# Feed-forward layers of a fused attention kernel: five nearly equal token blocks, and second products begun two tiles into the next block

## The chip, the cores and the metric

The kernel runs on one core of a Trainium2 chip. The metric is the time of one execution in device microseconds (us); the kernel before takes 1122.49 us, the median of 3 runs (1120.99 to 1125.56).

## The reference

Causal attention with per-position decay (4 batches, 8 heads, 576 positions, 64 wide) gives x, 2304 tokens by 512. Two feed-forward layers follow, all in float32:

```
def _moe_ref(x, w_in, w_out):            # w_in 512 x 2048, w_out 2048 x 512
    h = x @ w_in
    g = h * (1.0 / (1.0 + np.exp(-1.702 * h)))
    return g @ w_out

def _moe2_ref(x, w_gate, w_val, w_out):  # 512 x 1536, 512 x 1536, 1536 x 512
    g = x @ w_gate
    silu = g * (1.0 / (1.0 + np.exp(-g)))
    return silu * (x @ w_val) @ w_out
```

## The kernel before, in words

Attention comes first and is ordered by a planner of its own (class `Program`); the change does not touch it. The feed-forward layers are the function `moe`. There the tokens are the moving columns of each matmul, cut into five blocks, and the 128 x 128 weight pieces are stationary. A float32 operand is split into a high and a low part, so each product is three matmuls (lines 512 to 514: high x high, high weight x low, low weight x high).

The hidden features are cut into tiles of 128 and the tiles into chunks: four chunks of four tiles in layer 1, four of three in layer 2. For each chunk and each block the loop at line 579 runs over the chunk's tiles. A tile is a `first` product (line 516: 12 matmuls in layer 1; in layer 2 two of them, 24 matmuls), then the gate (line 529: ACT's tanh into `t`, DVE's multiplication into `s`), in layer 2 one more multiplication (line 546), and `split_g` (line 522: ACT's cast gives the high part of `g`, DVE's subtraction the low part). When all tiles of a block are made, the block is kept in `pend`. Its second products, `flush` (line 568), run inside the next block: 48 matmuls in layer 1, 36 in layer 2, in four groups by output tile `d`, each group followed on DVE by an addition to `acc` (lines 557 and 559). PE's order inside a flush may mix the four groups.

Weights arrive as float64 or float32 bit patterns and are converted on the way (`load_w`, line 449): ACT line 461, four DVE steps (lines 463 to 468), ACT's cast (line 481) and POOL's subtraction (line 482) give a `w` tile of a high and a low part. There are 13 such tiles; `pump` moves the conversions forward between tiles and flush groups, and a weight's place comes free when its last reader is done. A last block's flush frees the second weights of its chunk.

The lines that set when a flush runs are these:

```
for i in range(c, e):
    gs.append(layer1(i, t0, n) if lay == 1 else layer2(i, t0, n))
    ...
    if pend is not None:
        flush(pend)
        pend = None
    pump()
```

So PE has one tile of the next block as cover between the end of a block's last tile and the first use of its `g`.

Of the kernel before, what the change touches and what calls it, by code (L numbers as in the profile page):

```python
# [7 lines left out]
F32 = mybir.dt.float32  # L8
F32R = mybir.dt.float32r
# [99 lines left out]
def kernel(  # L109
# [13 lines left out]
    NW = 13  # L123
    NWA = 5
    NSTG = 3
    blocks = [(0, 512), (512, 512), (1024, 256), (1280, 512), (1792, 512)]

    def f32(ap):
        return ap.bitcast(F32)

    def pool(stack, name, bufs, **kw):
        return stack.enter_context(tc.tile_pool(name=name, bufs=bufs, **kw))
# [290 lines left out]
    def chunks(sizes):  # L423
        c = 0
        for n in sizes:
            yield c, c + n
            c += n
# [56 lines left out]
    def pump(force=False):  # L484
        for g in list(pipe):
            if next(g, "end") == "end":
                pipe.remove(g)
        if plan and len(pipe) < NSTG and (force or work[0] >= due[plan[0]]):
            pipe.append(load_w(plan.pop(0)))
            next(pipe[-1])  # L490

    def need(*keys):
        while not all(k in wt for k in keys):
            pump(True)

    def drop(*keys):
        for k in keys:
            del wt[k]
            live[0] -= 1

    def moe():
        gp = pool(ctx, "gp", 5, reuse_waits="tile")
        tp = pool(ctx, "tp", 2, reuse_waits="tile")
        ps = pool(ctx, "ps", 8, reuse_waits="tile", **psum)
        mp = pool(ctx, "mp", 1, reuse_waits="tile")
        acc = [mp.tile([128, KD, n], F32, name=f"acc{i}") for i, (_, n) in enumerate(blocks)]

        def mm3(o, pairs):
            n = len(pairs)
            work[0] += 3 * n * o.shape[1]  # L510
            for i, (wh, wl, rh, rl) in enumerate(pairs):
                nc.tensor.matmul(o, wh, rh, start=i == 0, stop=False)  # L512
                nc.tensor.matmul(o, wh, rl, start=False, stop=False)  # L513
                nc.tensor.matmul(o, wl, rh, start=False, stop=i == n - 1)  # L514

        def first(w, t0, n):
            o = ps.tile([128, 512], F32, tag="ps", name="ps")
            mm3(o[:, 0:n], [(w[:, 0, k * 128:(k + 1) * 128], w[:, 1, k * 128:(k + 1) * 128],
                             xhi[:, k, t0:t0 + n], xlo[:, k, t0:t0 + n]) for k in range(KD)])
            return o[:, 0:n]  # L520

        def split_g(s):
            n = s.shape[1]
            g = gp.tile([128, 2, 512], F32R, tag="g", name="g")
            nc.scalar.copy(out=g[:, 0, 0:n], in_=s)  # L525
            nc.vector.tensor_tensor(out=g[:, 1, 0:n], in0=s, in1=f32(g[:, 0, 0:n]), op=ALU.subtract)  # L526
            return g

        def gated(o, scale):
            n = o.shape[1]  # L530
            t = tp.tile([128, 512], F32, tag="t", name="t")[:, 0:n]
            nc.scalar.activation(out=t, in_=o, func=AF.Tanh, scale=scale)  # L532
            s = tp.tile([128, 512], F32, tag="s", name="s")[:, 0:n]
            nc.vector.scalar_tensor_tensor(out=s, in0=t, scalar=1.0, in1=o, op0=ALU.add, op1=ALU.mult)  # L534
            return s

        def layer1(i, t0, n):
            need(("w1", i))
            return split_g(gated(first(wt["w1", i], t0, n), 0.851))

        def layer2(i, t0, n):
            need(("wg", i), ("wv", i))
            g_ = first(wt["wg", i], t0, n)
            v_ = first(wt["wv", i], t0, n)
            s = gated(g_, 0.5)
            nc.vector.tensor_tensor(out=s, in0=s, in1=v_, op=ALU.mult)  # L546
            return split_g(s)

        def second(name, c0, gs, bi, d, mode):
            t0, n = blocks[bi]  # L550
            o = ps.tile([128, 512], F32, tag="ps", name="ps")[:, 0:n]
            ds = slice(d * 128, (d + 1) * 128)
            mm3(o, [(wt[name, c0 + i][:, 0, ds], wt[name, c0 + i][:, 1, ds], g[:, 0, 0:n], g[:, 1, 0:n])
                    for i, g in enumerate(gs)])
            a = acc[bi][:, d, :]
            if mode == "first":
                nc.vector.tensor_scalar(out=a, in0=o, scalar1=0.5, scalar2=None, op0=ALU.mult)
                return
            nc.vector.scalar_tensor_tensor(out=a, in0=o, scalar=0.5, in1=a, op0=ALU.mult, op1=ALU.add)  # L559
            if mode == "x":  # L560
                nc.scalar.copy(out=xhi[:, d, t0:t0 + n], in_=a)
                nc.vector.tensor_tensor(out=xlo[:, d, t0:t0 + n], in0=a, in1=f32(xhi[:, d, t0:t0 + n]), op=ALU.subtract)
            elif mode == "out":
                nc.sync.dma_start(out=out[ds, t0:t0 + n], in_=a)

        pend = None

        def flush(p):
            name, c0, gs, bi, mode, keys = p
            need(*[(name, c0 + i) for i in range(len(gs))])  # L570
            for d in range(KD):
                second(name, c0, gs, bi, d, mode)
                pump()
            if keys:
                drop(*keys)

        for lay, ff, sizes, name2 in ((1, FF1, CH1, "w1o"), (2, FF2, CH2, "w2o")):
            for c, e in chunks(sizes):
                for bi, (t0, n) in enumerate(blocks):
                    lastb = bi == len(blocks) - 1  # L580
                    gs = []
                    for i in range(c, e):
                        gs.append(layer1(i, t0, n) if lay == 1 else layer2(i, t0, n))
                        if lastb:
                            if lay == 1:
                                drop(("w1", i))
                            else:
                                drop(("wg", i), ("wv", i))
                        if pend is not None:
                            flush(pend)  # L590
                            pend = None
                        pump()
                    mode = "first" if c == 0 else "mid" if e < ff else "x" if lay == 1 else "out"
                    pend = (name2, c, gs, bi, mode, [(name2, i) for i in range(c, e)] if lastb else None)
        flush(pend)
# [18 lines left out]
    for _ in range(3):  # L614
        pump()
    moe()


# [48 lines left out]
```

## Time and profile before

| | before |
|---|---|
| median of 3 runs | 1122.49 us |
| the profiled execution, device time | 1123.12 us |
| its span in the trace | 1121.1 us |
| first and last matmul of the feed-forward layers start at | 265.77 and 1116.96 us |
| busy: PE, DVE, ACT, POOL | 94%, 56%, 32%, 16% of the span |

The span is the time from the first to the last instruction; the device time holds some 2 us around it. Matmuls are pipelined: one that lasts 0.39 us in a row is followed by the next after 0.23 us. So a loss on PE is read from the starts of two matmuls and the number of matmuls between them, not from busy time. A bracket at a row's end gives the time for which the engine sat idle before the row and what ended it.

### The profile page before, as it was taken

The numbers are of one execution on the slowest core, as the hardware profiler recorded it, in microseconds if no ns is written. First come the engines' busy times: TensorE is split into PE (matmuls) and PEld (weight loads), VectorE is DVE, ScalarE is ACT, GpSimd is POOL, SyncE is SP. The second block draws the span as 40 slices with busy tenths as digits, with TensorE's granted clock in tenths as the row PEclk, the third lists the DMA queues.
The fourth block names the chain that finished last, engine by engine and source line by source line (L and its number), as shares of the span: only waits on it lengthen the run. The fifth ranks groups of instructions, "written<-read, shape, count | busy, mean of one in ns | idle before, by whom it ended". The sixth has DMA issues, their size and how long they took to land.

```text
span 1121.1 us, 15630 instructions
## 1 busy us (share of the span) xinstructions
PE 1048.3 (94%) x6212; PEld 860.2 (77%) x6212; DVE 623.2 (56%) x1227; ACT 360.8 (32%) x648; POOL 182.4 (16%) x262
## 2 busy tenths in 40 slices
PE   2888777889999999999999999999999999999998
PEld 1666656667688788878877888888888888888886
DVE  5456756552966835664485578337733863363333
ACT  1455444443524313332343343123212321221110
POOL 4333343331201100200020011002100210010000
PEclk9999888999999999999999999999999999999999
DMA  3133353210221300220021012002200220000101
GB/s 121 45 103 114 97 165 105 96 47 23 79 72 38 113 1 1 75 75 1 19 95 37 1 57 95 1 1 77 93 1 1 88 82 1 1 0 29 48 19 75
DMA packets 25464, 61.43 MB, mean 55 GB/s; under 512 B 7760, under 2 KB 8272, under 8 KB 25392
## 3 DMA queue, kind: packets, MB, share of 16 engines
q1 hardware_dynamic: 25392, 60.45, 17.0%
q8 instruction: 48, 0.79, 0.3%
q14 instruction: 24, 0.20, 0.1%
HBM read 55.35 MB, written 4.94 MB: 54 GB/s over the span
## 4 chain that ended last, share of the span: by engine, by line
PE 80%; DVE 12%; ACT 2%; issue 2%; DMA 2%; POOL 1%; SPq 1%; ACTq 0%; DVEq 0%; POOLq 0%
PE ps L513 22%; PE ps L514 22%; PE ps L512 22%; PE sc L326 5%; PE xx L356 4%; PE mx L272 2%; DVE cvt L466 2%; DVE junk L279 2%; PE xx L385 2%; DVE cvt L468 2%; PE mx L275 1%; DVE cvt L464 1%; DVE cvt L463 1%; DVE g L526 1%; DVE s L534 1%
## 5 line engine op out<-in xcount | busy, mean ns | idle before, releaser
L512 PE MATMUL ps<-xhi,w 128*128 128x512 f32 (+1 forms) x800 | 294.5, 368 | 0.0
L513 PE MATMUL ps<-xlo,w 128*128 128x512 f32 (+1 forms) x800 | 294.4, 368 | 0.0
L514 PE MATMUL ps<-xhi,w 128*128 128x512 f32 (+1 forms) x800 | 294.2, 368 | 0.0
L513 PE MATMUL ps<-g,w 128*128 128x512 f32 (+1 forms) x560 | 207.5, 371 | 3.1 <-DVE g L526 3.1
L512 PE MATMUL ps<-g,w 128*128 128x512 f32 (+1 forms) x560 | 206.1, 370 | 3.7 <-ACT g L525 3.6
L514 PE MATMUL ps<-g,w 128*128 128x512 f32 (+1 forms) x560 | 206.1, 368 | 0.5 <-POOL w L482 0.5
L482 POOL TENSOR_TENSOR w<-cvt,w 128x512 fp32r<-128x512 f32 x68 | 89.4, 1319 | 664.8 <-ACT w L481 648.4
L532 ACT ACTIVATE t<-ps 128x512 f32<-128x512 f32 (+1 forms) x140 | 77.5, 554 | 298.4 <-PE ps L514 297.5
L512 PEld LDWEIGHTS ps<-xhi,w 128*128 128x128 f32 x800 | 150.8, 189 | 25.2
L514 PEld LDWEIGHTS ps<-xhi,w 128*128 128x128 f32 x800 | 150.8, 188 | 25.1
L513 PEld LDWEIGHTS ps<-xlo,w 128*128 128x128 f32 x800 | 150.8, 189 | 24.9
L534 DVE SCALAR_TENSOR_TENSOR s<-t,ps 128x512 f32<-128x512 f32 (+1 forms) x140 | 88.4, 631 | 123.9 <-ACT t L532 123.0
L525 ACT CAST g<-s 128x512 fp32r<-128x512 f32 (+1 forms) x140 | 81.0, 578 | 182.9 <-DVE s L546 129.4
L513 PEld LDWEIGHTS ps<-g,w 128*128 128x128 f32 x560 | 105.6, 189 | 24.5 <-DVE g L526 7.4
L512 PEld LDWEIGHTS ps<-g,w 128*128 128x128 f32 x560 | 105.4, 189 | 24.6 <-ACT g L525 7.3
L559 DVE SCALAR_TENSOR_TENSOR acc<-ps,acc 128x512 f32<-128x512 f32 (+1 forms) x120 | 76.0, 636 | 84.9 <-PE ps L514 84.2
L526 DVE TENSOR_TENSOR g<-s,g 128x512 fp32r<-128x512 f32 (+1 forms) x140 | 92.0, 658 | 54.1 <-ACT g L525 53.4
L514 PEld LDWEIGHTS ps<-g,w 128*128 128x128 f32 x560 | 105.6, 189 | 17.9 <-POOL w L482 0.9
L279 DVE CUSTOM_DVE_ANT_0 junk<-mx,maskw 128x512 bf16<-128x512 f32 (+3 forms) x128 | 61.8, 483 | 38.2 <-PE mx L275 36.2
L331 ACT ACTIVATE p<-sc 128x512 f32<-128x512 f32 (+2 forms) x128 | 56.4, 504 | 34.9 <-PE sc L326 34.6
L335 POOL TENSOR_SCALAR_AFFINE_SELECT p<-p 128x128 f32<-128x128 f32 (+1 forms) x160 | 43.9, 290 | 144.7 <-ACT p L331 143.6
L546 DVE TENSOR_TENSOR s<-s,ps 128x512 f32<-128x512 f32 (+1 forms) x60 | 38.0, 633 | 46.0 <-PE ps L514 45.7
(70 smaller groups left out, 1029.5 us busy)
## 6 DMA issues: line engine op xcount, KB each, us to landing
raw<-in_kq_dram SPq DMA_DIRECT2D x16, 576.0 KB
stg<-in_w_dram SPq DMA_DIRECT2D x16, 512.0 KB
stg<-in_w1o_dram SPq DMA_DIRECT2D x16, 512.0 KB
stg<-in_wg_dram SPq DMA_DIRECT2D x12, 512.0 KB
stg<-in_wv_dram SPq DMA_DIRECT2D x12, 512.0 KB
stg<-in_w2o_dram SPq DMA_DIRECT2D x12, 512.0 KB
vr<-in_v_dram SPq DMA_DIRECT2D x16, 320.0 KB
rb<-rw SPq DMA_DIRECT2D x32, 144.0 KB
```

Source lines behind the costliest of these rows:

```text
L279: nc.vector.tensor_tensor_reduce(out=junk[:, 0:n], in0=mx[:, e * 512 + o:e * 512 + o + n], in1=maskw[:, end - n:end], scale=1.0, scalar=fl ...
L326: nc.tensor.matmul(bank[e][:, o:o + n], w[half[e]], x[half[e]], start=w.tensor is h_.tensor and x.tensor is h_.tensor, stop=x.tensor is sm ...
L331: nc.scalar.activation(out=ps[e][:, a:z], in_=sc[c % 2][e][:, 0:z - a], func=AF.Exp, scale=0.125)
L482: nc.gpsimd.tensor_tensor(out=w[:, 1, :], in0=st, in1=f32(w[:, 0, :]), op=ALU.subtract)
L512: nc.tensor.matmul(o, wh, rh, start=i == 0, stop=False)
L513: nc.tensor.matmul(o, wh, rl, start=False, stop=False)
L514: nc.tensor.matmul(o, wl, rh, start=False, stop=i == n - 1)
L525: nc.scalar.copy(out=g[:, 0, 0:n], in_=s)
L526: nc.vector.tensor_tensor(out=g[:, 1, 0:n], in0=s, in1=f32(g[:, 0, 0:n]), op=ALU.subtract)
L532: nc.scalar.activation(out=t, in_=o, func=AF.Tanh, scale=scale)
L534: nc.vector.scalar_tensor_tensor(out=s, in0=t, scalar=1.0, in1=o, op0=ALU.add, op1=ALU.mult)
L559: nc.vector.scalar_tensor_tensor(out=a, in0=o, scalar=0.5, in1=a, op0=ALU.mult, op1=ALU.add)
```

## The change

The blocks become 462, 462, 460, 460 and 460 tokens instead of 512, 512, 256, 512 and 512. The tiles of `g`, `t` and `s` are 462 wide instead of 512. A pending flush runs only from the second tile of the next block on, and `g` has six buffers instead of five. From line 127 on, line numbers are one higher than before.

```
-    blocks = [(0, 512), (512, 512), (1024, 256), (1280, 512), (1792, 512)]
+    BLK = 462
+    blocks = [(0, 462), (462, 462), (924, 460), (1384, 460), (1844, 460)]
...
-        gp = pool(ctx, "gp", 5, reuse_waits="tile")
+        gp = pool(ctx, "gp", 6, reuse_waits="tile")
...
-            g = gp.tile([128, 2, 512], F32R, tag="g", name="g")
+            g = gp.tile([128, 2, BLK], F32R, tag="g", name="g")
...
-            t = tp.tile([128, 512], F32, tag="t", name="t")[:, 0:n]
+            t = tp.tile([128, BLK], F32, tag="t", name="t")[:, 0:n]
...
-            s = tp.tile([128, 512], F32, tag="s", name="s")[:, 0:n]
+            s = tp.tile([128, BLK], F32, tag="s", name="s")[:, 0:n]
...
-                        if pend is not None:
+                        if pend is not None and i > c:
                             flush(pend)
                             pend = None
                         pump()
```

PE at the first flush of all, before; `xhi` and `xlo` are the tokens, `w_1139` is the weight of the chunk's first tile:

```order
L512 MATMUL ps_2832<-xhi_58,w_1139 128x512
L513 MATMUL ps_2832<-xlo_59,w_1139 128x512
L514 MATMUL ps_2832<-xhi_58,w_1139 128x512
L512 MATMUL ps_2852<-g_2750,w_1646 128x512
L512 MATMUL ps_2866<-g_2750,w_1646 128x512
L512 MATMUL ps_2880<-g_2750,w_1646 128x512
```

PE at the same place after the change; `w_1291` is the weight of the chunk's second tile:

```order
L513 MATMUL ps_2852<-xhi_58,w_1291 128x462
L514 MATMUL ps_2852<-xlo_59,w_1291 128x462
L515 MATMUL ps_2852<-xhi_58,w_1291 128x462
L513 MATMUL ps_2872<-g_2750,w_1646 128x462
L513 MATMUL ps_2886<-g_2750,w_1646 128x462
L513 MATMUL ps_2902<-g_2750,w_1646 128x462
```

The flush now stands behind the next block's second tile, 12 matmuls later in layer 1; the number of matmuls, 4080 in the two layers, stays.

ACT at that first flush, before; `g_2829` is the last tile of the block that is flushed, `w_2809` the last weight that the flush needs, `t_2845` the first tile of the next block:

```order
L525 CAST g_2806<-s_2804 128x512
L532 ACTIVATE t_2845<-ps_2832 128x512
L525 CAST g_2829<-s_2827 128x512
L481 CAST w_2809<-cvt_2760 128x512
L461 ACTIVATE cvt_2961<-stg_2939 128x512
L525 CAST g_2849<-s_2847 128x512
```

ACT there after the change:

```order
L526 CAST g_2806<-s_2804 128x462
L533 ACTIVATE t_2845<-ps_2832 128x462
L526 CAST g_2829<-s_2827 128x462
L533 ACTIVATE t_2865<-ps_2852 128x462
L482 CAST w_2809<-cvt_2760 128x512
L462 ACTIVATE cvt_2981<-stg_2959 128x512
```

The tanh of the next block's second tile, `t_2865`, has moved ahead of the last weight's cast.

ACT at the opening of chunk 2, where the last block of chunk 1 is flushed, before; `w_3791` and `w_3830` are casts into places which that flush frees, the rows ahead of them belong to the opening's first tile:

```order
L532 ACTIVATE t_3477<-ps_3464 128x512
L525 CAST g_3481<-s_3479 128x512
L481 CAST w_3791<-cvt_3729 128x512
L481 CAST w_3830<-cvt_3794 128x512
L461 ACTIVATE cvt_3833<-stg_3814 128x512
L461 ACTIVATE cvt_3858<-stg_3853 128x512
L532 ACTIVATE t_3553<-ps_3540 128x512
```

ACT there after the change:

```order
L533 ACTIVATE t_3477<-ps_3464 128x462
L526 CAST g_3481<-s_3479 128x462
L533 ACTIVATE t_3497<-ps_3484 128x462
L526 CAST g_3501<-s_3499 128x462
L482 CAST w_3811<-cvt_3749 128x512
L482 CAST w_3850<-cvt_3814 128x512
L462 ACTIVATE cvt_3853<-stg_3834 128x512
```

The second tile's tanh and cast (`t_3497`, `g_3501`) now stand ahead of the two casts that wait for the flush.

## Rows read from the trace of the kernel before

**Rows 1.** The page: span, and busy time of PE.

```profile
span 1121.1 us, 15630 instructions
PE 1048.3 (94%) x6212; PEld 860.2 (77%) x6212; DVE 623.2 (56%) x1227; ACT 360.8 (32%) x648; POOL 182.4 (16%) x262
```

**Rows 2.** The page: granted TensorE clock in 40 slices, tenths of full speed.

```profile
PEclk9999888999999999999999999999999999999999
```

**Rows 3.** PE's waits from 266 us on: total us, times, longest.

```profile
PE ps L512 <- ACT g L525: 3.6, 6, 1.0
PE ps L513 <- DVE g L526: 3.1, 8, 0.5
```

**Rows 4.** Groups by shape on PE: busy us, mean ns of one | idle before.

```profile
L512 PE MATMUL ps<-xhi,w 128*128 128x512 f32 x640 | 249.3, 390 | 0.0
L512 PE MATMUL ps<-xhi,w 128*128 128x256 f32 x160 | 45.2, 282 | 0.0
L512 PEld LDWEIGHTS ps<-xhi,w 128*128 128x128 f32 x800 | 150.8, 189 | 25.2
```

**Rows 5.** Timeline of PE, undisturbed runs: start us, duration us, engine, instruction.

```profile
311.09 0.39 PE L514 MATMUL ps<-g,w 128*128 128x512 f32 x1
...
316.53 0.39 PE L514 MATMUL ps<-g,w 128*128 128x512 f32 x1
316.76 0.28 PE L512 MATMUL ps<-xhi,w 128*128 128x256 f32 x1
...
320.95 0.28 PE L514 MATMUL ps<-xhi,w 128*128 128x256 f32 x1
```

**Rows 6.** Timeline of PE from the layers' start through the first flush.

```profile
265.77 0.50 PE L512 MATMUL ps<-xhi,w 128*128 128x512 f32 x1
...
279.28 0.39 PE L514 MATMUL ps<-xhi,w 128*128 128x512 f32 x1
...
285.61 0.96 PE L512 MATMUL ps<-g,w 128*128 128x512 f32 x3 [0.57 <-ACT g L525]
...
289.12 0.50 PE L514 MATMUL ps<-g,w 128*128 128x512 f32 x1 [0.47 <-POOL w L482]
...
293.77 0.39 PE L512 MATMUL ps<-xhi,w 128*128 128x512 f32 x1
```

**Rows 7.** Timelines of DVE, ACT and POOL at the first flush: its last weight.

```profile
286.03 0.68 DVE L468 SCALAR_TENSOR_TENSOR cvt<-stg,cvt 128x512 uint32<-128x512 uint32 x1
286.74 0.62 ACT L481 CAST w<-cvt 128x512 fp32r<-128x512 f32 x1
287.44 1.62 POOL L482 TENSOR_TENSOR w<-cvt,w 128x512 fp32r<-128x512 f32 x1 [3.41 <-ACT w L481]
```

**Rows 8.** Timeline of PE in the second flush, behind the first 256-wide tile.

```profile
308.00 0.50 PE L513 MATMUL ps<-g,w 128*128 128x512 f32 x1 [0.40 <-DVE g L526]
```

**Rows 9.** Timeline of PE at the opening of chunk 2: both flushes' stops.

```profile
364.85 0.50 PE L513 MATMUL ps<-g,w 128*128 128x512 f32 x1 [0.18 <-DVE g L526]
...
387.30 0.50 PE L512 MATMUL ps<-g,w 128*128 128x512 f32 x1 [0.53 <-ACT g L525]
388.32 0.50 PE L513 MATMUL ps<-g,w 128*128 128x512 f32 x1 [0.51 <-DVE g L526]
```

**Rows 10.** Timelines of POOL and DVE at that opening: a conversion beside POOL.

```profile
381.57 1.29 POOL L482 TENSOR_TENSOR w<-cvt,w 128x512 fp32r<-128x512 f32 x1 [1.35 <-issue]
381.74 1.40 DVE L464 TENSOR_SCALAR cvt<-cvt 128x512 uint32<-128x512 uint32 x1
...
386.51 0.42 DVE L464 TENSOR_SCALAR cvt<-cvt 128x512 uint32<-128x512 uint32 x1
```

**Rows 11.** Groups by shape on DVE from 266 us on: the gate's multiplication.

```profile
L534 DVE SCALAR_TENSOR_TENSOR s<-t,ps 128x512 f32<-128x512 f32 x112 | 76.6, 684 | 112.7 <-ACT t L532 112.6
L534 DVE SCALAR_TENSOR_TENSOR s<-t,ps 128x256 f32<-128x256 f32 x28 | 11.7, 419 | 11.2 <-ACT t L532 10.4
```

**Rows 12.** Timeline at the end: the last addition.

```profile
1117.39 0.69 DVE L559 SCALAR_TENSOR_TENSOR acc<-ps,acc 128x512 f32<-128x512 f32 x1 [1.35 <-PE ps L514]
```

## The prediction, made before the change was run

> **What bounds the kernel now.** I read the page first: a span of 1121.1 us in which PE is busy for 94% [rows 1]; the reader should take from it only that PE is the engine to look at, since a matmul row outlasts the distance to the next one. The granted clock comes next: it leaves its upper level (2.4 GHz) in three slices early in attention, and the slices of the feed-forward layers, the 256-wide blocks and all their stops included, stand at full [rows 2]. Then the distance between starts in undisturbed runs [rows 5]: 24 matmuls of 512 columns take 316.53 - 311.09 = 5.44 us, 0.2267 each; 35 of 256 columns take 4.19 us, 0.1197 each. The line through both is 0.4167 ns a column (one column per cycle at 2.4 GHz) and 13.3 ns a matmul. Last the waits of PE in the layers: the high part of `g` from ACT 3.6 us in 6 stops, the low part from DVE 3.1 us in 8 [rows 3], and next to nothing else.
>
> So the layers are a stream of 4080 matmuls with a few stops. How much do these cost? A stop costs more than its bracket: the row ahead of it lasts 0.39 us where its successor would have begun after 0.23, and the first row after it lasts 0.50 instead of 0.39, as in [rows 9]; that is 0.16 + 0.11 = 0.27 us on top.
>
> - First flush: from 265.77 to 293.77 us there are 60 + 48 matmuls of 512, 24.5 us of work in 28.0 us [rows 6]: 3.5 us lost.
> - Second flush, behind the first 256-wide tile: from 293.77 us to the row at 316.76 us [rows 5, 6] there are 84 of 512 and 12 of 256, 20.5 us of work in 23.0 us: 2.5 us lost; the stop at 308.00 is its last one [rows 8].
> - Opening of chunk 2 [rows 9]: 0.18 + 0.27 = 0.45 us in the flush of the old chunk's last block, and 0.53 + 0.51 + 2 x 0.27 = 1.6 us in the flush of the new chunk's first block. The openings of chunks 3 and 4 repeat this pattern, so 3 x 2.05 = 6.2 us.
>
> Together 12.2 us. As a check, the 14 stops of [rows 3] give 6.7 + 14 x 0.27 = 10.5 us, without those too short to leave a bracket. Layer 2 has no stop worth a row: its tile is 24 matmuls, and that cover has sufficed, behind a 256-wide tile too (2.9 us).
>
> **The change part by part.** *New blocks.* Each of the 816 matmuls per block exists five times before and after. By the line, one of each block costs 4 x 226.7 + 120 = 1027 ns before and 2 x 205.8 + 3 x 205.0 = 1027 ns after: nothing. No row shows a matmul of 460 or 462 columns, so I bound its deviation from the line: it lies between two measured widths, and I take 0; for the range I allow 1 ns either way, 4 us on 4080 matmuls. The weight load is no floor: its rows last 189 ns [rows 4], yet 256-wide matmuls, each with its own load, start every 120 ns.
>
> *Gate, split and additions.* Their number is the same. DVE's step goes from 419 ns at 256 to 684 at 512 [rows 11], 1.035 ns a column, so about 632 at 462; the sum over five blocks is unchanged. They lie beside PE's work. At the end the last addition is 0.05 us shorter [rows 12] and the store behind it a tenth smaller: I take 0.1 us.
>
> *The later flush.* The cover between a block's last tile and the first use of its `g` was 12 matmuls in layer 1: 2.72 us behind a 512-wide tile, 1.44 behind a 256-wide one. It becomes 24 x 0.205 = 4.9 us everywhere, 2.2 or 3.5 us more.
> - Second flush: late by 2.5, cover up by 3.5: gone.
> - Openings: late by 1.6 and 0.45, cover up by 2.2: gone, with 0.6 us to spare if DVE's and ACT's order stayed. It does not stay, and the move helps: the opening's second tile has its tanh and cast ahead of the two casts that wait for the flush, as ACT's order shows, so less is queued ahead of the last `g`. Against that stands that those casts, and the conversions behind them, still start only when the flush is nearly done.
> - First flush: here the cover is not what ends the wait. Its last stop, at 289.12 us, waits for POOL's half of the last second weight [rows 6], whose chain is DVE 286.03, ACT 286.74, POOL 287.44 to 289.06 [rows 7]. After the change the same ten DVE rows stand ahead of it, six of them on tiles and 0.05 us shorter: DVE 0.3 us earlier. But on ACT the tanh of the next block's second tile (0.55 us by its shorter width) now stands ahead of the cast. So POOL ends at about 289.3, and PE goes on at 289.4 at the earliest, with 18 matmuls of the flush left by its new order: 289.4 + 0.1 + 18 x 0.2058 = 293.2 us. Without any stop it would be there at 265.8 + 0.1 + 120 x 0.2058 = 290.6. So 2.6 of the 3.5 us stay: PE merely comes later to a wait that ends when it ended. From below this could be 0.9 us gained, from above all 3.5.
>
> *Six `g` buffers and freed places.* The third tile of a block takes a place that the flush frees; its 12 matmuls (2.5 us) run behind the flush's last reading, so ACT's cast into it comes later anyway. The second weights' places come free one tile later, but the casts that wait for them are for the next chunk but one, which PE needs some 90 us later. What that could cost is only ACT's queue, in the first rival.
>
> Sum: 12.2 - 2.6 = 9.6 us gained, with the end's 0.1 us 9.7. The profiled execution had a span of 1121.1 us and a device time of 1123.1; it becomes 1111.4 and 1113.4. It stood 0.6 us above the median of 1122.5, so against the median I forecast 1112.8 us.
>
> **Weighed against the skill.** At the openings DVE's conversion step took 1.40 us beside POOL's subtraction of 1.29 us, ending with it, where the same step takes 0.42 us at 386.51 us with POOL idle [rows 10]. The Trainium skill ("SBUF — State Buffer", "Who interferes with whom") says that VectorE and GpSimd share one pair of ports, locked for a whole instruction, and that a VectorE instruction with two SBUF inputs is caught by it as well as the fast copies. The row agrees. By that rule the subtraction that makes the low part of `g` can be held for most of a POOL instruction, which is more than the 0.6 us that I have to spare; this is part of the first rival.
>
> **The rivals.**
> 1. *The stop at each opening persists.* Mechanism: the conversions behind the waiting casts move with the flush, DVE is as full ahead of the last `g`, and one step held for 1 us beside POOL [rows 10] uses up the margin. For it: the chain is tied to the flush, and the scheduler's order is made without that holding. Against: two tile steps and part of two conversions have left the queue ahead of that `g`. Price: 3 x 1.6 = 4.8 us stay, so 4.9 are gained: 1117.6 us.
> 2. *All stops go.* The mixed order of the first flush lets PE run while the last weight is made. For it: ACT's delay by one tanh is an estimate, and its queue has gaps there. Against: the weight's chain has not become shorter. 12.3 us gained: 1110.2 us.
> 3. *Slower: a matmul of odd width or start costs more than the line.* Its place is every matmul of the layers. All token blocks of before start at multiples of 256 columns, those of after at 462, 924, 1384 and 1844, and the low part of `g` at column 462 of its tile; nothing in the rows excludes that such reads cost some cycles. From 9.7 us / 4080 = 2.4 ns per matmul on it turns the gain into a loss. At 6 ns, half of the fixed 13.3, it is 24.5 us, and the result 1137 us. Against it: the line is exact at both widths, which leaves no sign of a cost by width. The Trainium skill ("TensorE: Matmul & The Clock Gate", "Why this matters for your kernels") advises dimensions of 512 and more, since narrow products can let the clock fall. In this trace the 256-wide blocks ran at the full grant [rows 2], so I give that next to nothing and let it stand inside this rival.
>
> **How the numbers follow.** Forecast 65% (own range 1111 to 1115), first rival 17%, second 11%, third 7%. The range that should hold 8 of 10 takes the forecast, the second rival and about half of the first: 1109.8 to 1117.6 us; of the 4 us for an unknown cost by width it takes in the loss and most of the gain. A difference of 0.5%, 5.6 us, is about what a measurement of this kernel can tell from none (single runs lie 4.6 us apart). The forecast and the second rival are below 1116.9, and a third of the first: 0.82 faster. The rest of the first and a little of the third are within: 0.12. The third gives 0.06 slower.
>
> **What would show it.** Undisturbed matmuls of 462 columns should start every 0.206 us; 0.208 or more speaks for the third rival. The waits of PE should fall from 7 us to about 2, nearly all in the first flush, and a stop on POOL's half of the last weight should still stand near 289 us. At the openings no row of PE with `g` should carry a bracket; two of about 0.5 us each would be the first rival. The forecast is wrong if the distance between starts is off the line, or if a new wait shows on PE (for a weight, or for a place in PSUM) that before does not have.

## The result and the profile after

The changed kernel takes 1128.8 us (median of 6 runs, 1127.0 to 1130.5), the kernel before, measured with it, 1121.7 us (6 runs, 1120.1 to 1125.7). The ratio is 1.0056, with a 95% interval of 1.0033 to 1.0080: slower by 7 us, where 1112.8 us and a gain of 9.7 us were forecast. It lies outside the range; the third rival happened.

The page of the changed kernel, to be read beside [rows 1, 2]: span, busy times, granted clock.

```profile
span 1125.8 us, 15621 instructions
...
PE 1060.6 (94%) x6212; PEld 917.0 (81%) x6212; DVE 624.6 (55%) x1227; ACT 359.9 (32%) x648; POOL 184.7 (16%) x262
...
PEclk9999898999999999999999999999999999999999
```

PE's share is the same, and the clock stands at its upper level (2.4 GHz) from the eighth slice to the end, so the clock explains nothing. The busy times of PE and PEld have risen, but their rows overlap and don't say by how much the path has grown.

PE's waits from 262 us on, to be read beside [rows 3]: total us, times, longest.

```profile
PE ps L513 <- ACT g L526: 0.7, 1, 0.7
PE ps L515 <- POOL w L483: 0.3, 1, 0.3
```

The waits are gone as forecast: 1.0 us in 2 stops, where before had the 6.7 in 14 of [rows 3] and one of 0.5 on POOL. Whoever looked at waits alone would expect a gain. The distance between starts tells the rest. PE in an undisturbed stretch of a 460-wide block, to be read beside [rows 5]:

```profile
339.26 0.37 PE L513 MATMUL ps<-xhi,w 128*128 128x460 f32 x1
...
340.52 0.37 PE L513 MATMUL ps<-g,w 128*128 128x460 f32 x1
...
342.82 0.37 PE L515 MATMUL ps<-g,w 128*128 128x460 f32 x1
```

Six first products take 1.26 us and the eleven second ones behind them 2.30 us: 0.210 and 0.209 us each, where the line gives 205.0 ns for 460 columns. Over the whole layers the first products stand at 209 to 213 ns, the second ones at 207 to 211, different from block to block and, but for the first chunk, much alike from chunk to chunk. Two more stretches of the same view, in chunk 2: the block that starts at column 0, and the one that starts at 924.

```profile
371.21 0.37 PE L513 MATMUL ps<-xhi,w 128*128 128x462 f32 x1
...
375.02 0.37 PE L513 MATMUL ps<-xhi,w 128*128 128x462 f32 x1
...
411.71 0.38 PE L513 MATMUL ps<-xhi,w 128*128 128x460 f32 x1
...
415.55 0.38 PE L513 MATMUL ps<-xhi,w 128*128 128x460 f32 x1
```

Each pair is eighteen distances apart: 211.7 ns at 462 columns, 213.3 at 460.

The account, from PE's first to its last start in the layers. Timeline of before, the last matmul (the first is in [rows 6]):

```profile
1116.96 0.39 PE L514 MATMUL ps<-g,w 128*128 128x512 f32 x1
```

Timeline of after, the first and the last matmul of the layers:

```profile
263.28 0.47 PE L513 MATMUL ps<-xhi,w 128*128 128x462 f32 x1
...
1121.75 0.37 PE L515 MATMUL ps<-g,w 128*128 128x460 f32 x1
```

| us | before | after | difference |
|---|---|---|---|
| first to last start | 851.19 | 858.47 | +7.28 |
| of it lost in stops (by how much the distances at each stop exceed the usual one) | 12.57 | 1.84 | -10.7 |
| the rest, 4079 distances | 838.6 (205.6 ns each) | 856.6 (210.0 ns each) | +18.0 |

So 10.7 us were gained and 18.0 us, 4.4 ns per matmul, were paid. The spans differ by only 4.7 us because attention ended 2.5 us earlier in this one execution; the medians differ by 7.1 us, as the layers do.

The first flush after, PE, DVE, ACT and POOL, to be read beside [rows 6, 7]:

```profile
278.37 0.37 PE L515 MATMUL ps<-xhi,w 128*128 128x462 f32 x1
...
283.06 0.69 PE L513 MATMUL ps<-g,w 128*128 128x462 f32 x2 [0.72 <-ACT g L526]
...
282.85 0.68 DVE L469 SCALAR_TENSOR_TENSOR cvt<-stg,cvt 128x512 uint32<-128x512 uint32 x1
283.81 0.57 ACT L533 ACTIVATE t<-ps 128x462 f32<-128x462 f32 x1
284.26 0.63 ACT L482 CAST w<-cvt 128x512 fp32r<-128x512 f32 x1
284.97 1.29 POOL L483 TENSOR_TENSOR w<-cvt,w 128x512 fp32r<-128x512 f32 x1 [3.14 <-ACT w L482]
...
286.31 0.47 PE L515 MATMUL ps<-g,w 128*128 128x462 f32 x1 [0.25 <-POOL w L483]
```

The tanh of the next block's second tile stands ahead of the last weight's cast, and POOL ends just as PE goes on, both as forecast. PE loses 1.5 us here (0.9 at 283.06, where 1.09 us lie between two starts instead of 0.21, then 0.4, and 0.1 behind each of the two stops), where 2.6 was forecast. Of the difference of 1.1 us, some 0.6 come from the weight's chain. Measured from the layers' first start, DVE's last step began 0.7 us earlier than before instead of 0.3, and POOL's row took 1.29 us instead of 1.62. The other 0.5 is no merit of the flush: at 4.9 ns more for each of the 102 matmuls ahead of it, PE came to the stop later.

PE after at the opening of chunk 2, the flush of the new chunk's first block, to be read beside [rows 9]:

```profile
380.69 0.37 PE L513 MATMUL ps<-g,w 128*128 128x462 f32 x1
...
387.87 0.37 PE L514 MATMUL ps<-g,w 128*128 128x462 f32 x1
```

There is no bracket: 34 distances in 7.18 us, 211 ns each, as everywhere in this block. DVE after just ahead of it, to be read beside [rows 10]:

```profile
376.41 1.60 DVE L527 TENSOR_TENSOR g<-s,g 128x462 fp32r<-128x462 f32 x1
...
379.71 1.40 DVE L465 TENSOR_SCALAR cvt<-cvt 128x512 uint32<-128x512 uint32 x1
381.03 0.63 DVE L527 TENSOR_TENSOR g<-s,g 128x462 fp32r<-128x462 f32 x1
```

What the first rival spoke of did happen, twice. The subtraction that makes the low part of `g` took 1.60 us at 376.41, for the block's third tile, instead of 0.63. The conversion step right ahead of the last tile's subtraction (381.03) took 1.40 us at 379.71 instead of 0.42. But the longer cover took both in.

### The profile page after: what moved, and what is told of

Its sections match the earlier page's. It is cut to its first block, busy times and chain, and to the rows that moved or that the text cites. A ratio compares the mean times of both kernels' runs of the same rounds, so it can differ in the third digit from the quotient of the medians.

```text
span 1125.8 us, 15621 instructions
## 1 busy us (share of the span) xinstructions
PE 1060.6 (94%) x6212; PEld 917.0 (81%) x6212; DVE 624.6 (55%) x1227; ACT 359.9 (32%) x648; POOL 184.7 (16%) x262
## 4 chain that ended last, share of the span: by engine, by line
PE 89%; DVE 4%; issue 3%; DMA 1%; ACT 1%; POOL 1%; SPq 0%; DVEq 0%; POOLq 0%; ACTq 0%
PE ps L515 25%; PE ps L514 25%; PE ps L513 25%; PE sc L327 5%; PE xx L357 3%; PE mx L273 2%; DVE junk L280 2%; PE xx L386 2%; PE mx L276 1%; PE mx L309 1%; ACT selm L312 1%; DMA stg<-in_w1o_dram 1%; DVE cvt L469 0%; SPq L185 0%; DMA rs<-ss 0%
## 5 line engine op out<-in xcount | busy, mean ns | idle before, releaser
L515 PE MATMUL ps<-xhi,w 128*128 128x460 f32 (+1 forms) x800 | 298.1, 373 | 0.0
L514 PE MATMUL ps<-xlo,w 128*128 128x460 f32 (+1 forms) x800 | 298.0, 373 | 0.0
L513 PE MATMUL ps<-xhi,w 128*128 128x460 f32 (+1 forms) x800 | 297.8, 372 | 0.0
L515 PE MATMUL ps<-g,w 128*128 128x460 f32 (+1 forms) x560 | 207.9, 372 | 0.3 <-POOL w L483 0.3
L514 PE MATMUL ps<-g,w 128*128 128x460 f32 (+1 forms) x560 | 207.8, 371 | 0.0
L513 PE MATMUL ps<-g,w 128*128 128x460 f32 (+1 forms) x560 | 206.9, 371 | 0.7 <-ACT g L526 0.7
L483 POOL TENSOR_TENSOR w<-cvt,w 128x512 fp32r<-128x512 f32 x68 | 91.7, 1352 | 667.5 <-ACT w L482 649.0
L533 ACT ACTIVATE t<-ps 128x460 f32<-128x460 f32 (+1 forms) x140 | 77.4, 554 | 288.7 <-PE ps L515 288.7
L535 DVE SCALAR_TENSOR_TENSOR s<-t,ps 128x460 f32<-128x460 f32 (+1 forms) x140 | 88.3, 631 | 112.1 <-ACT t L533 111.7
L526 ACT CAST g<-s 128x460 fp32r<-128x460 f32 (+1 forms) x140 | 80.8, 578 | 184.6 <-DVE s L547 135.0
L527 DVE TENSOR_TENSOR g<-s,g 128x460 fp32r<-128x460 f32 (+1 forms) x140 | 96.9, 693 | 59.2 <-ACT g L526 58.6
L560 DVE SCALAR_TENSOR_TENSOR acc<-ps,acc 128x460 f32<-128x460 f32 (+1 forms) x120 | 76.0, 636 | 88.2 <-PE ps L515 88.2
L547 DVE TENSOR_TENSOR s<-s,ps 128x460 f32<-128x460 f32 (+1 forms) x60 | 37.9, 632 | 50.7 <-PE ps L515 50.4
```

Of the source, the lines that this page charges most:

```text
L483: nc.gpsimd.tensor_tensor(out=w[:, 1, :], in0=st, in1=f32(w[:, 0, :]), op=ALU.subtract)
```

## The experiments

Four ideas why the distance is off the line stood at the start: A, widths and starts that aren't multiples of 16 columns; B, the width as such; C, the other engines' traffic; and D, something in the later flush. The expectations use these letters.

**The distance by itself.** Behind the last flush of the kernel before, 27 streams of 36 matmuls each, with `xhi` and `xlo` as both operands and nothing else running; `n` is the width, `t0` the first column of the moving rows, `w0` of the stationary ones:

```
+        def stream(n, t0, w0=0):
+            for r in range(3):
+                o = ps.tile([128, 512], F32, tag="ps", name="ps")[:, 0:n]
+                mm3(o, [(xhi[:, k, w0 + r * 128:w0 + (r + 1) * 128], xlo[:, k, w0 + r * 128:w0 + (r + 1) * 128],
+                         xhi[:, k, t0:t0 + n], xlo[:, k, t0:t0 + n]) for k in range(KD)])
...
+        for n, t0, w0 in PROBE:
+            stream(n, t0, w0)
```

> The kernel before with 27 bare streams of 36 matmuls each behind its last flush (three matmuls per pair as in the layers, nothing on DVE, ACT or POOL beside them); the streams differ in width, in the column at which the moving rows start, and in two cases in the column of the stationary piece. It adds some 205 us; what counts is the distance between starts in each stream. Theory A (a moving row that does not begin and end on a multiple of 16 float32 columns costs extra): 384, 448, 464, 480, 496 and 512 from column 0 lie on the line 13.3 ns + 0.4167 ns a column (173.3, 200.0, 206.7, 213.3, 220.0, 226.7 ns), while 456, 460, 462, 472, 504 and 508 lie 1 to 6 ns above their line, and a width of 512 or 464 or 480 started at column 4, 8 or 14 also lies above. Theory B (the width comes near the 189 ns of the weight load, and the two disturb each other): everything from 448 to 480 lies about 5 ns above the line whatever its start, 384, 496 and up lie on it. Theory C (the 5 ns come from the traffic of DVE, ACT and POOL beside the matmuls): all streams lie on the line, 462 at 205.8.

Measured, mean distance in ns once a stream has settled, which takes up to a dozen matmuls (in brackets: above the line of 13.3 + n/2.4), `w0` = 0 unless said:

| n, from column 0 | 384 | 448 | 456 | 460 | 462 | 464 | 480 | 496 | 504 | 512 |
|---|---|---|---|---|---|---|---|---|---|---|
| ns | 173.3 (0) | 206.7 (6.7) | 208.6 (5.3) | 206.7 (1.7) | 211.5 (5.7) | 210.2 (3.5) | 216.5 (3.2) | 220.0 (0) | 226.7 (3.3) | 226.7 (0) |

460 from column 924 took 213.3, 462 from 462 209.9; 512 from column 4 took 231.6, from 8 233.3; 512 with only the stationary rows moved by 4 took 233.3. Some starts were cheaper: 462 from column 8 took 206.7, as did 460 from 4, but 460 from 8 and from 16 211.2. PE of this kernel, 462 from column 0 and 460 from column 924:

```profile
1145.43 0.38 PE L517 MATMUL ps<-xhi 128*128 128x462 f32 x1
...
1149.24 0.38 PE L517 MATMUL ps<-xhi 128*128 128x462 f32 x1
...
1246.30 0.38 PE L517 MATMUL ps<-xhi 128*128 128x460 f32 x1
...
1250.14 0.38 PE L517 MATMUL ps<-xhi 128*128 128x460 f32 x1
```

Eighteen distances take 3.81 and 3.84 us, as in the two blocks of the changed kernel with these widths and starts. The third start that was tried, 462 from 462, gave 209.9 here and 209.5 to 210.2 there. So these first products run at the distance that their width and start have by themselves, with nothing beside them (the first chunk differs: the block at 924 took 210.0 there). The eight streams not listed lie 3 to 8 ns above the line.

So C falls (nothing else ran), A falls as it stood (448, 464 and 480 are multiples of 16 and off the line), and B alone falls as well, since 512 is on or off the line by its start.

**Blocks that are multiples of 32**, with the later flush.

```
-    BLK = 462
-    blocks = [(0, 462), (462, 462), (924, 460), (1384, 460), (1844, 460)]
+    BLK = 480
+    blocks = [(0, 480), (480, 480), (960, 448), (1408, 448), (1856, 448)]
```

> The changed kernel with blocks of 480, 480, 448, 448 and 448 tokens and tiles of 480, all widths and starts multiples of 16 columns; the later flush stays. Theory A: matmuls start every 213.3 and 200.0 ns, on the line; the 20 us are gone and the stops stay away, so 1109 to 1113 us, about 17 us less than the changed kernel. Theory B: both widths stay some 5 ns over the line, 1127 to 1131 us, no difference from the changed kernel. Theory C: the same as B.

Measured: 1127.7 us, ratio to before 1.0050 (1.0033 to 1.0067). The 480-wide matmuls stand at 217 to 219 ns (+3 to +6), the 448-wide at 203 to 207 (+3 to +7). That misses A's time and is where B and C expected it.

**The new blocks with the old flush.**

```
-                        if pend is not None and i > c:
+                        if pend is not None:
```

> The changed kernel with the flush again behind the first tile of the next block; blocks of 462 and 460 stay, six buffers of g too. All theories of the matmul's width: matmuls still start every 210 to 211 ns (so the distance does not come from the later flush), and the stops of before return, shortened where the 256-wide block was: 5 to 10 us of stops against 1.8 in the changed kernel, so 1132 to 1139 us. If the distance falls to 205 to 206 ns, the later flush is what stretches the matmuls (rival), and the time is 1115 to 1120 us.

Measured: 1139.4 us, ratio 1.0152 (1.0121 to 1.0183). PE's waits of this kernel from 262 us on:

```profile
PE ps L513 <- ACT g L526: 5.1, 6, 1.8
PE ps L514 <- DVE g L527: 3.3, 7, 0.6
```

The distances are those of the changed kernel, 207 to 213 ns, and the stops are back: 12.7 us lost by the starts, more than the 5 to 10 that were expected. D falls, and the later flush is worth 1139.4 - 1128.8 = 10.6 us.

**Tiles of 464 instead of 462**, so that the low part of `g` starts at column 464.

```
-    BLK = 462
+    BLK = 464
```

> The changed kernel with the tiles of g, t and s 464 columns wide, of which 462 or 460 are used as before; token blocks unchanged. So the rows of g begin at multiples of 16 columns in both parts, those of x stay where they were. Theory A: second products (g) fall to 206 to 208 ns in all blocks (in the changed kernel 207 to 212), first products (x) stay at 210 to 212; 2 to 5 us less, 1124 to 1127 us. Theories B and C: no difference, 1127 to 1131 us.

Measured: 1126.0 us, ratio 1.0041 (1.0012 to 1.0071). From first to last start 856.2 us (in an execution whose attention ended 12.5 us later), 2.2 us less than after, and not in the second products alone: the first products, whose starts among the tokens are the same, moved as well, most in the block at column 924, from 212.8 to 206.7 ns in layer 1. So width and start alone don't fix the distance. The 462-wide second products only fell from 211 to 210 ns, where A had 206 to 208. The time is within A's range, its reason isn't borne out, and the intervals of the two kernels overlap: inconclusive.

**The later flush alone, on the old blocks.** To make room for a sixth `g` of 512, `s` is written over `t`, with three buffers for both.

```
-        gp = pool(ctx, "gp", 5, reuse_waits="tile")
-        tp = pool(ctx, "tp", 2, reuse_waits="tile")
+        gp = pool(ctx, "gp", 6, reuse_waits="tile")
+        tp = pool(ctx, "tp", 3, reuse_waits="tile")
...
-            s = tp.tile([128, 512], F32, tag="s", name="s")[:, 0:n]
+            s = t
...
-                        if pend is not None:
+                        if pend is not None and i > c:
```

> The kernel before, its blocks of 512 and 256 kept, with only the later flush and six buffers of g; to find room for the sixth, the gate's product is written over its tanh tile (three buffers instead of two and two). Theory A2 (what the changed kernel loses is the distance between matmuls of 462, 460, 448 and 480 columns, and the later flush takes the stops away): matmuls of 512 and 256 start every 226.7 and 120.0 ns as before, the stops fall from 12.6 us to 1 to 3, so 9 to 11 us less than before, 1110 to 1113 us. Rival (the later flush itself spoils the stream, through what then runs beside it): distances above 228 ns, and the time within 3 us of before.

Measured: 1108.65 us (6 runs), ratio 0.9867 (0.9836 to 0.9898). This version beats both kernels, and is 1.4 us below the range that was expected. Its page:

```profile
span 1109.6 us, 15613 instructions
```

PE's waits of this kernel from 262 us on:

```profile
PE ps L514 <- POOL w L482: 0.5, 1, 0.5
PE ps L512 <- ACT g L525: 0.3, 1, 0.3
```

Its timeline of PE in an undisturbed stretch:

```profile
308.67 0.39 PE L514 MATMUL ps<-g,w 128*128 128x512 f32 x1
...
311.85 0.39 PE L513 MATMUL ps<-g,w 128*128 128x512 f32 x1
```

Fourteen distances in 3.18 us are 227 ns: the line holds again. The layers take 839.7 us from first to last start, with 1.5 us of stops. So the two halves of the change are told apart: the flush gives 11 us, the blocks take 18. That `s` lies over `t` here is no part of the gain, as far as can be told: the kernel with the old flush, where `t` and `s` are apart, prices the flush at 10.6.

**The same with the 256-wide block last**, to see whether its cover still matters.

```
-    blocks = [(0, 512), (512, 512), (1024, 256), (1280, 512), (1792, 512)]
+    blocks = [(0, 512), (512, 512), (1024, 512), (1536, 512), (2048, 256)]
```

> As the run with the later flush alone, with the 256-wide block as the last of the five. Theory A2: the same distances and stops; the end is shorter, since the last addition and the last store are half as wide (0.3 us and some tenths), so equal to the later flush alone within 2 us, at best 1 us less. Rival: a 256-wide last block gives the flush less cover at each opening of a chunk (24 x 0.12 = 2.9 us behind it, where the conversions crowd), so stops of 0.5 to 1.5 us per opening return, 2 to 4 us more than the later flush alone.

Measured: 1109.05 us, ratio 0.9878 (0.9848 to 0.9908), with 1.4 us of stops. No difference from the version above that could be told.

**Before, with its tokens moved by 4 columns**, all widths and the order kept.

```
-    xhi = xp.tile([128, KD, NT], F32R, name="xhi")
-    xlo = xp.tile([128, KD, NT], F32R, name="xlo")
+    xhi = xp.tile([128, KD, NT + 16], F32R, name="xhi")[:, :, 4:NT + 4]
+    xlo = xp.tile([128, KD, NT + 16], F32R, name="xlo")[:, :, 4:NT + 4]
```

> The kernel before with the tiles of the tokens 16 columns wider per row and used from column 4 on, so that every first product's moving rows begin 4 columns off; nothing else changes. Theory A2 (start counts): first products of 512 go from 226.9 to about 231.6 ns as in the bare stream from column 4, second products (g) stay; 1920 x 4.7 ns = 9 us for the 512-wide ones, the 256-wide ones add 0 to 3: 1129 to 1134 us. Theory B (width alone counts): no change, 1120 to 1123 us.

Each partition holds four such rows one behind the other, one for each 128 of the 512 features. As each is 16 columns longer, the four are moved by 4, 20, 36 and 52 columns, and not all by 4.

Measured: 1133.4 us, ratio 1.0075 (1.0050 to 1.0100): slower by the starts alone, and within what was expected if they count. PE of this kernel, a second flush's last matmul and the first products behind it:

```profile
332.05 0.28 PE L514 MATMUL ps<-g,w 128*128 128x256 f32 x1
332.17 0.40 PE L512 MATMUL ps<-xhi,w 128*128 128x512 f32 x1
332.41 0.39 PE L513 MATMUL ps<-xlo,w 128*128 128x512 f32 x1
332.64 0.39 PE L514 MATMUL ps<-xhi,w 128*128 128x512 f32 x1
332.87 0.40 PE L512 MATMUL ps<-xhi,w 128*128 128x512 f32 x1
```

The moved 512-wide first products start every 231 to 233 ns instead of 227; the second products, whose operands were not moved, are at 227 to 230, 0.5 ns more in the mean than before. The moved 256-wide ones got faster, 118 to 119 ns, which nobody expected.

**More widths and starts by themselves**, streams as in the first probe.

> The kernel before with 31 bare streams of 36 matmuls behind its end: widths 256 to 512 in steps of 16 from column 0, then 512 started at column 16, 32, 64, 128, 448 at 16, 32, 64, 448, and the stationary piece moved by 16, 32 and 64 columns for both. Theory A2 with a unit of 16 columns: every multiple of 16 in start keeps 512 on 226.7 ns and 448 on 206.7. With a larger unit: starts of 16 and 32 lift 512 to 230 ns and more, 128 does not. Theory B (width against the weight load): the widths above the line form one band around 448 to 480, the others lie on it, and no start matters. A third reading (the distance comes in steps of 16 columns, 6.67 ns, and rounds up): every distance in a steady stream is a multiple of 6.67 ns.

Measured, ns (above the line), all from column 0 unless said: 256 120.0 (0), 272 to 304 1.4 to 2.1 below the line, 320 to 400 on it, 416 188.4 (1.8), 432 196.2 (2.8), 448 202.8 (2.8), 464 208.8 (2.2), 480 216.5 (3.2), 496 220.0 (0), 512 226.7 (0). 512 from column 16 took 228.9, from 32 232.3, from 64 and from 128 226.7. Moving only the stationary rows by 16, 32 and 64 gave 233.2, 232.3 and 226.7. So for 512 the distance is back on the line at a move of 64 columns (256 bytes), for either operand.

For 448 it is another pattern: from column 64 and from 448 it took 206.7, from 32 203.9, and from 16 200.0, on the line; with only the stationary rows moved by 16, 32 and 64 it took 202.2, 204.0 and 206.7. PE of this kernel, 448 from column 16, eighteen distances in 3.60 us:

```profile
1258.29 0.36 PE L519 MATMUL ps<-xhi 128*128 128x448 f32 x1
...
1261.89 0.36 PE L519 MATMUL ps<-xhi 128*128 128x448 f32 x1
```

None of the three readings holds as it stood: the unit of 16 falls by 512 from column 16, B by the starts, and steps of 6.67 ns by 188.4 or 202.8.

**Is it the start of each operand, or how the two stand to one another?** Streams with both starts given.

> The kernel before with 29 bare streams of 36 matmuls behind its end, some with the moving rows and the stationary piece moved by the same number of columns. Theory P (what counts is where the two starts lie to each other, modulo 64 columns): 512 with both at 4, 8, 16, 32 or 48, or at 32 and 96, lies on 226.7 ns, with one of them moved by 32 or 48 at 230 to 235. Theory Q (what counts is each start by itself, on the grid of 64 columns): all of these lie 2 to 7 ns above the line but those whose starts are both multiples of 64. Theory R (the distance of one stream depends on what ran before it): 448 from column 0, run three times behind different streams, gives different distances, between 200 and 207 ns; by P and Q it gives one. 384 and 256 from columns 4, 16, 32 and 64 show whether narrow blocks are free of it: by all three 64 lies on the line (173.3 and 120.0).

Measured for 512, first columns of moving and stationary rows:

| both moved alike | 4, 4 | 8, 8 | 16, 16 | 32, 32 | 48, 48 | 32, 96 | 96, 32 |
|---|---|---|---|---|---|---|---|
| ns | 230.1 | 227.1 | 226.8 | 227.4 | 227.4 | 226.7 | 226.7 |

| one moved | 0, 32 | 32, 0 | 48, 0 |
|---|---|---|---|
| ns | 233.5 | 233.5 | 233.2 |

How the two starts stand to one another, modulo 64 columns, decides for 512, with (4, 4) as a part miss. That equal starts are the good ones holds for 512 alone: 448 with both at 16 or both at 32 took 206.7, and 460 with both at 32 208.9, 3.9 above the line. Narrow blocks aren't free of the start either: 384 took 175.5 from column 4 and 176 from 32, and 173.3, the line, from 16 and 64; 256 took 113.3, 117.8, 118.8 and 120.0 from 4, 16, 32 and 64. 496 from 32 took 226.7, 6.7 above the line, while 496 from 496 and 400 from 400 lie on it.

PE of this kernel, 512-wide streams with starts 0 and 32, then 448 from 0 and 0 twice (1225.12 behind a stream of 512, 1238.68 behind one of 384), then 256 from column 4 and from column 64:

```profile
1169.46 0.40 PE L520 MATMUL ps<-xhi 128*128 128x512 f32 x1
...
1170.85 0.40 PE L520 MATMUL ps<-xhi 128*128 128x512 f32 x1
...
1225.12 0.36 PE L520 MATMUL ps<-xhi 128*128 128x448 f32 x1
...
1226.33 0.37 PE L520 MATMUL ps<-xhi 128*128 128x448 f32 x1
...
1238.68 0.36 PE L520 MATMUL ps<-xhi 128*128 128x448 f32 x1
...
1239.91 0.37 PE L520 MATMUL ps<-xhi 128*128 128x448 f32 x1
...
1271.24 0.28 PE L520 MATMUL ps<-xhi 128*128 128x256 f32 x1
...
1271.92 0.28 PE L520 MATMUL ps<-xhi 128*128 128x256 f32 x1
...
1283.82 0.28 PE L520 MATMUL ps<-xhi 128*128 128x256 f32 x1
...
1284.53 0.28 PE L520 MATMUL ps<-xhi 128*128 128x256 f32 x1
```

Each pair is six distances apart: 1.39, 1.21, 1.23, 0.68 and 0.71 us. These are the first six of each stream; once settled, the streams stand at 233.5, 202.8, 206.7, 113.3 and 120.0 ns. The same 448-wide stream has two distances, so P can't be the whole of it, and R's sign is there: a stream settles into one of several rhythms. What chooses among them is not shown. The streams ahead differ (behind 512 from column 48 it was 206.7), but so do the PSUM buffers that are written, as each stream takes the next three of eight.

## Why the prediction was wrong

- **The step that failed is "New blocks": by the line, nothing, with 1 ns either way.** It was 4.4 ns per matmul, 18.0 us instead of 0 ± 4. The line came from two widths that were both measured at starts on multiples of 256 columns [rows 5], and it was taken to hold between them because 460 lies between 256 and 512. The bare streams show that it doesn't: from column 0, 256, 320 to 400, 496 and 512 are on it, 416 to 480 are not, and with one operand moved 512 isn't either. "It lies between two measured widths" was no bound: the rows showed neither a width between nor another start. The sign that was named for it, 0.208 us or more at 462 columns, is there: 0.210 to 0.212.
- **The third rival had the right place, every matmul of the layers, and the right point from which it decides** (2.4 ns per matmul), but 7% was too little. Its mechanism, odd widths or starts, is half of what was found: 448 and 480, multiples of 32, cost as much as 460 and 462. "The line is exact at both widths" was given as evidence against it; two points always lie on a line, so it was none. Its price by 6 ns, 1137 us, was too high by a third: 4.4 ns.
- **The later flush was right.** The second flush's stop and the openings' are gone; the stops fell by 10.7 us where 9.6 was forecast. The difference is the first flush, 1.5 us left instead of 2.6: in part DVE and POOL were there earlier than the estimate, in part it is luck, since the longer matmuls brought PE to the stop later. The version with the later flush alone gains 12.7 us in the medians, of which the stops are 11.1.
- **The first rival** did not happen, though two DVE steps were held beside POOL at the opening of chunk 2 (1.60 and 1.40 us): the cover sufficed. The second rival did not happen: a stop on POOL's half of the last weight still stands.
- **The clock** stayed at its full grant (9 tenths or more in every slice of the layers), so a falling clock, which the third rival also weighed, had no part in the loss.

That the loss is the distance between matmuls, and that the distance goes by width and start with nothing else running, is shown. That other things count as well is shown too: with tiles of 464, the block at 924 has the same width and start and another distance. What makes the distance is not shown. That the reads of the moving rows meet those of the next weights fits one thing: for 512 columns the relation of the two starts decides, and moving only the stationary rows, of which each matmul loads new ones, costs as much as moving the tokens. The Trainium skill ("TensorE: Matmul & The Clock Gate", "Step-by-step: what each phase is for") says that loading weights through a port of its own takes no read bandwidth from the running matmul. These runs don't fit that as it stands: with the stationary start alone moved by 32 columns, 512 goes from 226.7 to 232.3 or 233.5 ns, and with both moved by 32 it is back at 227.4. Which reads meet where, no run shows. Open stay why 448 has two rhythms, why 256 gets faster from column 4, and which part of the 4.4 ns the second products owe to the places of `g` and the weights. No kernel that cures the 460-wide blocks by placing alone was built: tiles of 464 got back 2 us of 18, and the cheaper starts of the bare streams (462 from 8, 460 from 4, 448 from 16) were not tried in the layers.

## What to carry to other kernels

A cost per matmul read at two widths holds for these widths at these starts; before a stream of thousands is cut anew, measure the new width at its new start by itself, because 4.4 ns times 4080 (18 us) outweighs all the stops of this profile together (12.6 us). Prefer cuts whose distance has been measured to be on the line (here 512 and 256 at multiples of 64 columns), even if they are uneven. And where a change has two parts, price and try them apart: here the later flush alone, on the old blocks, is the best version, 1108.65 us.

## What the runs showed of the hardware that was not expected

- The distance of 512-wide matmuls depends on how the first columns of moving and stationary rows stand to one another modulo 64 columns: 226.7 to 227.4 ns when equal (at 4 and 4 it was 230.1), 228.9 to 233.5 when not. For 448 equal starts are not the fast ones: 202.8 or 206.7 ns, against 200.0 with the moving rows 16 columns on.
- From column 0 the widths 416 to 480 cost 1.7 to 6.7 ns above the line, 504 takes 3.3 more, and 272 to 304 up to 2.1 ns less.
- 256 columns from column 4 take 113.3 ns, 6.7 below the 120.0 from columns 0 and 64: the fixed 13.3 ns of the line is no floor.
- The same stream can run at 202.8 or 206.7 ns (448 from 0 and 0), steady over some thirty matmuls; what decides between them is open.
